# A spectral filter and a SwiGLU block: the last step of the inverse transform on 32x32 tiles of TensorE, one burst a chunk, combined by GpSimd

## The chip, the cores and the metric

One Trainium2 chip, one NeuronCore of it. The metric is the device time of one execution in microseconds, taken as the median of several runs; beside the runs there is one execution recorded by the profiler, and all durations come from that one. The engines are called TensorE (PE in the profile, its weight loads PEld), VectorE (DVE), ScalarE (ACT), GpSimd (POOL) and SyncE (SP, which here only issues DMAs).

## The reference

```python
batch, seq, dim = (8, 3008, 256)          # n_freq = 1505
n_tokens, d_model, d_ff = (24064, 256, 1536)

def _attn_ref(x, filt_r, filt_i):
    X = np.fft.rfft(x, axis=1)
    F = (filt_r + 1j * filt_i)[None, :, :]
    Y = X * F
    y = np.fft.irfft(Y, n=x.shape[1], axis=1)
    return y.astype(np.float32)

def _moe_ref(x, w_gate, w_val, w_out):    # x: the filtered sequence, as 24064 tokens
    g = x @ w_gate
    silu = g * (1.0 / (1.0 + np.exp(-g)))
    val = x @ w_val
    return (silu * val @ w_out).astype(np.float32)
```

All of it is float32: a transform of length 3008 along the sequence of each of 8 batches, a pointwise product with a filter, the transform back, and then a gated feed-forward block over all tokens.

## The kernel before

**The transforms.** 3008 is 47 x 64 (`N1`, `N2`). The transform and its inverse are each made of a step over 64 and a step over 47, as small matrix products. For batch 0 the steps are done ahead and beside the first groups, in other functions (`stage1`, `stage2a`, `stage2b`, `stage3`), which the change leaves as they are. For batches 1 to 7 they are folded by symmetry and cut into pieces that TensorE does between the matmuls of the batch before: `quads` in steps 0 to 3 (L717, products `wqa`, on 24 rows x 32 columns of the array), `fours` in steps 4 to 10 (L797, products `wqc` and `wqb`, 64 x 64), and last `back` (L1031, products `wpd`), which turns the 24 real and 24 imaginary coefficients of each of 64 residues into 47 tokens. What `back` makes, `y`, is what the feed-forward block reads. `quads` and `fours` make the next batch, `back` mostly the batch that is being worked on.

**Chunks, groups, steps.** A batch is cut into 4 chunks of tokens (`NCHUNK`), the hidden dimension into 3 groups (`NG`). A step is one group of one chunk, so there are 12 steps a batch and 96 in all; step s of a batch is chunk s // 3 and group s % 3. A chunk's `y` tile is [128, 8, 188]: four parts of the tokens' values and four combinations of them.

**The order within a step** is written out by hand in `SCHEDULE` (L88), as a list of tokens that is walked once a step (L1502). All instructions are pinned: every engine does its own in the order in which the tokens issue them. A token with a prime belongs to the group of the step before. Those which matter here:

- `P0`..`Q3`, `A..`, `B..`, `E..`: the products of the hidden layer (L1125), by a scheme that needs fewer products than the plain one and more sums. `P`/`Q` read `y` and write banks `wk`; `A`, `B` write `wa`, `E` writes `we`.
- `f0`, `f1`, `f2`: ScalarE copies of `wk`; `D01`, `D02`, `D12`: their differences on GpSimd; `s..`, `x..`: sums on VectorE that start a bank `wa` (`s01` reads `D01`); `g`, `u`, `h`, `v`: the activation on ScalarE and its product on VectorE, into tiles `h`.
- `S00`, `S01`, `S10`, ... `S31` (L1173): sums and differences over the tiles `h`, on GpSimd. The first digit is the kind, the second one of the two tiles. S0 is an addition, and S1, S2 and S3 are subtractions that follow from it or from each other.
- `W1`..`W7`: the projection out (L1223, banks `wA`, `wF`, `wG`), two products each, one of each `h` tile. `W6` reads what `S10'` and `S11'` wrote, `W7` what `S20'` and `S21'` wrote.
- `o1`..`o7`: the projections' results are added into the output tile by VectorE; `x0.o` ..: stores of it.
- `n1`, `n2`, `n3`: sums over the next chunk's `y` (`combine_sequence`), on GpSimd, at the end of a chunk's last step.
- `b0`..`b7`: the next piece of the step's burst (`quads`, `fours`, or `first_fold` in step 11); `t0.0` .. `t4.3`: the next piece of one of the step's other pieces.

TensorE has eight PSUM banks, handed out in the order in which they come free.

**`back` before.** A chunk is made in two halves m = 0, 1. The table `back_t` holds for each half 32 of the 47 tokens, tokens 0 to 31 and tokens 15 to 46 (`LATER` is 15), so that 17 are made twice. The 48 coefficients, cosine and sine parts together, are one contraction of 48 rows; the two kinds h of residues lie at partitions 0 and 64. A half has 16 products into two banks, two transposes on VectorE (L1049) from the banks straight into `y`, and after the second half four small sums on GpSimd (128 x 188, `y<-y`). In steps 1, 4 and 7 the first half stands at `t2.0`, the second at `t3.1` (L1473), for the chunk that begins two steps later; chunk 0 of the next batch is done in step 11 from `t0.0` on (L1471). `load_t4` (L664) brings the coefficients of a chunk in two tiles, with two DMAs each on SyncE's queue. The tiles `x` of `xpool` (two buffers of [128, 512]) are used in batches 0 and 1 only.

Of the kernel before, what the change touches and what calls it, by code (L numbers as in the profile page):

```python
# [41 lines left out]
FP32 = mybir.dt.float32  # L42
# [43 lines left out]


SCHEDULE = """  # L88
Q0 o3' z1.o' t4.2' W2 b0 f0 S00' S01' i0 b1 b2 x0.o' t0.0 x1.o' i1 Q1 P0 t0.1 x2.o' P3 x3.o' f1 t4.3'
W1 x4.o' S10' x03 S11' D01 i2 i3 i4 s13 b3 x5.o' P1 o1 b4 t0.2 o2 z0.o c1 i5 A13 g1 c0 S20' Q2  # L90
S21' g0 y01 m13 t1.0 h0 f2 s01 W6 t1.1 h1 x23 D02 P2 o6 D12 A01 t0.3 i6 c2 i7 B13 i8 g2 i9 n3' m01
i10 S30' t1.2 i11 x02 W7 S31' g13 y12 y02 B01 h13 o7 t1.3 t2.0 s02 s12 g01 h2 b5 Q3 t2.1 h01 e12
A02 y23 W4 e02 b6 y03 m02 g3 A12 o4 z2.o t2.2 E12 m12 B02 t2.3 l12 e13 b7 E02 u12 g02 t3.0 h3 s23
l02 B12 v12 E13 t3.1 h02 u02 A23 n2 l13 g12 v02 W5 s03 e23 h12 e01 m23 A03 o5 z3.o u13 E23 t3.2 m03
v13 E01 l23 e03 t3.3 t4.0 l01 u23 B23 v23 u01 E03 n1 t4.1 v01 g23 B03 l03 W3 h23 g03 u03 h03 v03
""".split()
KS = (-1, 0, 1, 2)

# [15 lines left out]
LATER = N1 - 32  # L114

PIECES = ((0, 7), (7, 14), (14, 20), (20, 26))

# [4 lines left out]
def dft_tables():  # L122
# [27 lines left out]
    hi = 2 * np.pi * (np.outer(2 * n1 + 1, s) % (2 * N1)) / (2 * N1)  # L150
    scale = np.where(s == 0, 1.0, 2.0) / S
    one_hi = np.concatenate([np.cos(hi) * scale, -np.sin(hi) * scale * (s > 0)], 1).T
    back = np.zeros((128, 2, 32))
    for h, table in enumerate((one, one_hi)):
        for m in range(2):
            back[64 * h:64 * h + 2 * NS, m] = table[:, LATER * m:LATER * m + 32]
    back = back.reshape(128, 64)

    quad = np.zeros((4, 32, 2, 32))
    for h in range(2):  # L160
# [40 lines left out]
def kernel(  # L201
# [357 lines left out]
    def load_back():  # L559

        t = rpool.tile([128, 2, 128], U32, name="quad", tag="pw", bufs=3)
        t = t.bitcast(FP32).rearrange("p b f -> p (b f)")
        quad_t.append(t)
        pin(nc.sync.dma_start(out=t[:, 0:65], in_=quad_dram.ap()))
        t = rpool.tile([128, 2, 128, 2], U32, name="back", tag="raw", bufs=2)
        t = t.bitcast(FP32).rearrange("p b f two -> p (b f two)")
        back_t.append(t[:, 0:64])
        pin(nc.sync.dma_start(out=back_t[0], in_=back_dram.ap()))


# [1 line left out]
    def bank(name):  # L572
        return wps.tile([128, 512], FP32, name=f"w{name}", tag="w")
# [7 lines left out]
    class Spectral:  # L581
# [82 lines left out]
        def load_t4(self, k, i, part=None):  # L664
            at = 2 * k + i
            if part:
                self.load_rows(self.t4[k, i][8 * N_STORED:NK], k, slice(2 * N_STORED, NS), ts(i, NH))
                return
            t = t4pool.tile([128, NH, C], FP32, name=f"t4_{self.b}_{k}_{i}", tag="t4")
            if part == 0:  # L670
                self.load_rows(t[0:8 * N_STORED], k, slice(0, 2 * N_STORED), ts(i, NH), nc.gpsimd)
            elif self.b == 0:
                self.load_rows(t[0:NK], k, slice(0, NS), ts(i, NH))
            else:

                rows = self.d2_tokens.rearrange("(h n) a c -> h a n c", h=2)
                for h in range(2):
                    self.load(out=t[64 * h:64 * h + 2 * NS], in_=rows[h, :, ts(at, NH)])
            self.t4[k, i] = t

        def bank(self, name):
# [346 lines left out]

        def back(self, k, m):  # L1031

            if m == 0:
                self.y[k] = ypool.tile([128, 8, TQ], FP32, name=f"y_{self.b}_{k}", tag="y")
            y = self.y[k]
            banks = [bank(f"pd_{self.b}_{k}_{m}_{h}") for h in range(2)]
            outs_ = [t.rearrange("p (z i n d) -> p i z n d", z=2, i=2, d=32) for t in banks]
            for i in range(2):
                t = self.t4[k, i].rearrange("p n (z j d) -> p j z n d", z=2, d=32)
                for j in range(4):  # L1040
                    for h in range(2):
                        r = slice(64 * h, 64 * h + 2 * NS)
                        pin(nc.tensor.matmul(  # L1043
                            out=outs_[h][32 * j:32 * j + 32, i], lhsT=back_t[0][r, ts(m, 32)],
                            rhs=t[r, j], start=i == 0, stop=True, skip_group_check=True))
            yield
            to = y.rearrange("p s n -> p (s n)").rearrange("p (z h m r) -> p h z m r", z=2, h=2, r=N1)
            for h in range(2):
                pin(nc.vector.transpose(  # L1049
                    out=to[:, h, :, :, LATER * m:LATER * m + 32],  # L1050
                    in_=banks[h].rearrange("p (z m d) -> p z m d", z=2, d=32)))
                if h == 0:
                    yield
            for a in range(4 if m else 0):
                b, v = y[:, a], y[:, 4 + a]
                for _ in range(abs(KS[a])):
                    pin((sub if KS[a] > 0 else add)(nc.gpsimd, v, v, b))
# [33 lines left out]
    class Group:  # L1091
# [94 lines left out]
        def project(self, op, last=False):  # L1186
# [9 lines left out]
            if kind in "xXi":  # L1196
                t, cb, step = outs[b, k], int(kind == "X"), 2 if last else 1
                if kind == "x" and q < NG - 1 and takes_turns(b, k) and p == 5:
                    pin(nc.sync.dma_start(out=o_dram[k], in_=t))
                if q == NG - 1 and (b or kind == "i"):  # L1200
                    some = (p,) if kind == "i" else (2 * p, 2 * p + 1)
                    for n, (u, cq) in enumerate(divmod(m, 4) for m in some):
                        rows = min(32, NR - 32 * u)
                        at = (b * S + 32 * 32 * u + 2 * NH * k) * C + 128 * cb + 32 * cq
                        queue = nc.sync if b else nc.gpsimd
                        if last:
                            queue = (nc.sync, nc.scalar, nc.gpsimd)[(2 * p + n) % 3]
# [164 lines left out]


    older = before = None
    gap = iter(())
    pieces_before = []

    def order_of(b):
# [24 lines left out]
            yield  # L1403


    def later(piece):

        yield
        yield from piece

    def chain(*pieces):

# [30 lines left out]
    for b in range(B):  # L1443
# [2 lines left out]
        plan = [[] for _ in range(NCHUNK * NG)]  # L1446

        def three(s, k, cur=cur):
            if s.b == 0:
                return [s.stage3(k, step) for step in range(4)]  # L1450
            return [s.back(k, m) for m in range(2)]

        d = [three(cur, k) for k in range(1, NCHUNK)]
# [7 lines left out]
        if b + 2 < B:  # L1461
            bursts[-1] = following.first_fold()
        bursts = [iter(p) for p in bursts]
        two = []
        for u in range(N_TWO + 2) if b == 0 else ():
# [1 line left out]
            two += [nxt.stage2a(u)] if u < N_TWO else []  # L1467
        if nxt:
            gap = iter(())
            first = three(nxt, 0)  # L1470
            plan[11] = [first[0], gap, first[1]]  # L1471
            if b:
                plan[1], plan[4], plan[7] = [[gap, gap, p[0], later(p[1])] for p in d]  # L1473
            if b == 0:
                for k in range(NCHUNK - 1):
                    plan[k] = d[k] + one[k:k + 1]
                plan[0] = [gap, d[0][0], chain(d[0][1], d[0][2]), d[0][3], one[0]]
                plan[3], plan[4], plan[5] = one[3:8], one[8:13], one[13:16]
# [3 lines left out]
        else:  # L1482
            plan[1], plan[4], plan[7] = [[gap, gap, p[0], later(p[1])] for p in d]

        for step in range(NCHUNK * NG + (b == B - 1)):
            ghost = step == NCHUNK * NG
# [15 lines left out]
            for place, token in enumerate(SCHEDULE):  # L1502
# [51 lines left out]
                if op in ends and not last and (b or step >= NT * NG - 1):  # L1554
                    reload_weights((g + 1) % NG, ends[op])
            older, before, pieces_before = before, this, pieces
    for op in LAST:
        if op[0] == "S":
            older.step(op, nc.gpsimd if op[1] == "2" else nc.vector)
# [30 lines left out]
```

## Time and profile before

| What | Value |
|---|---|
| Median of 3 runs | 2785.24 us (2785.04 to 2791.29) |
| The profiled execution's own time | 2790.41 us |
| Its span, first to last instruction | 2788.6 us |
| Mean granted TensorE clock | 0.997 |
| L1043 weight loads, `wpd<-t,back` 48x32 | x1792, 27.5 us busy |
| L1049 VectorE transposes, `y<-wpd`, 128x512 | x112, 79.2 us busy, 707 ns each |
| L315 GpSimd `D<-f,f` 128x376 | x288, 280.5 us busy, 985 ns each |
| L877 GpSimd `lent<-lent` 128x512 | x48, 60.4 us busy, 1278 ns each |
| Time that GpSimd's `h` (L312) waited for VectorE's `h` | 402.2 us, 62 times |

A row of the groups reads: line, engine, operation, out <- in, partitions x elements, count, then busy time in us, the mean of one in ns, the idle time of the engine just before these instructions, and what ended it. Line numbers can be those of a helper: L312 is every addition, L315 every subtraction. A row of the timeline has the start in us, the duration of the merged run, the engine and the instruction. A row of windows has for each stretch its length, the busy time of PE, PEld, DVE, ACT and POOL with the number of instructions, the granted clock, the DMA share and GB/s. One product in float32 leaves two records on TensorE.

### The profile page before, as it was taken

What the parts mean: (1) busy time and instruction counts of PE and PEld (TensorE: products, weight loads), DVE (VectorE), ACT (ScalarE), POOL (GpSimd) and SP (SyncE); (2) the same over time, 40 slices, a digit from 0 to 9 for tenths busy, and PEclk for the clock granted to TensorE, in tenths of its full rate; (3) what the DMA queues carried; (4) which work ended last, traced back from release to release, by engine and by line L of the source; (5) the groups of instructions that cost most, each with busy time, mean ns of one, the idle gap of its engine ahead of it and who ended that gap; (6) DMA issues with size and microseconds to landing.
All of it is one profiled execution on the core that took longest, in us unless ns stands there. A gap on an engine that the chain in (4) does not pass through costs nothing.

```text
span 2788.6 us, 51410 instructions
## 1 busy us (share of the span) xinstructions
PE 2748.3 (99%) x16952; PEld 2249.3 (81%) x16952; DVE 2081.7 (75%) x4703; ACT 1514.6 (54%) x4086; POOL 1647.4 (59%) x1801
## 2 busy tenths in 40 slices
PE   8999999999999999999999999999999999999998
PEld 6777887888878888788878888878887888888886
DVE  7888777777687777777778777777777777676666
ACT  5776454555555555555555555555554555555553
POOL 4786576566545665556654566555655566555554
PEclk9999999999999999999999999999999999999999
DMA  8688877878676776777767777668767677655543
GB/s 216 218 273 267 282 240 243 265 243 263 205 211 208 253 244 190 212 238 229 247 184 233 220 249 223 207 194 264 243 213 201 215 239 237 183 156 147 156 137 83
DMA packets 383488, 608.47 MB, mean 218 GB/s; under 512 B 197118, under 2 KB 266652, under 8 KB 383048
## 3 DMA queue, kind: packets, MB, share of 16 engines
q1 hardware_dynamic: 364410, 574.18, 65.9%
q10 hardware_dynamic: 16174, 25.50, 3.6%
q0 software_dynamic: 2640, 5.51, 0.7%
q8 instruction: 137, 2.24, 0.3%
q14 instruction: 127, 1.04, 0.1%
HBM read 484.45 MB, written 118.12 MB: 216 GB/s over the span
## 4 chain that ended last, share of the span: by engine, by line
PE 89%; DVE 3%; POOL 2%; ACT 1%; DMA 1%; issue 1%; SPq 0%; POOLq 0%; DVEq 0%; ACTq 0%
PE wa L1125 25%; PE wk L1125 17%; PE wA L1223 16%; PE we L1125 12%; PE wG L1223 8%; PE wF L1223 4%; PE wpd L1043 2%; PE wqc L807 1%; PE wqb L819 1%; PE wqa L727 1%; POOL h L315 0%; POOL out_dram L1208 0%; PE wpa L889 0%; DVE we L315 0%; DVE y L319 0%
## 5 line engine op out<-in xcount | busy, mean ns | idle before, releaser
L1125 PE MATMUL wa<-y_t,wt_t 128*128 128x188 f32 x4464 | 883.5, 324 | 10.5 <-DVE wa L1147 5.5
L1125 PEld LDWEIGHTS wa<-y_t,wt_t 128*128 128x128 f32 x4464 | 746.0, 190 | 102.9 <-issue 14.7
L1125 PEld LDWEIGHTS wk<-y,wt_t 128*128 128x128 f32 x2976 | 494.4, 190 | 125.2 <-issue 36.7
L1125 PE MATMUL wk<-y,wt_t 128*128 128x188 f32 x2976 | 575.6, 326 | 1.4 <-ACT f L1140 1.4
L315 POOL TENSOR_TENSOR h<-h 128x376 f32<-128x376 f32 x572 | 560.1, 1000 | 15.1 <-DVE h L312 14.9
L1223 PE MATMUL wA<-h,wo_t 128*128 128x376 f32 x1532 | 549.0, 481 | 3.4 <-POOL h L315 1.8
L1125 PE MATMUL we<-y_t,wt_t 128*128 128x188 f32 x2232 | 432.4, 323 | 2.4 <-DVE we L319 1.6
L315 POOL TENSOR_TENSOR D<-f,f 128x376 f32<-128x376 f32 x288 | 280.5, 985 | 252.0 <-ACT f L1140 245.4
L312 POOL TENSOR_TENSOR h<-h 128x376 f32<-128x376 f32 x190 | 183.2, 984 | 408.0 <-DVE h L1172 402.2
L315 DVE TENSOR_TENSOR we<-we,m 128x376 f32<-128x376 f32 x576 | 317.3, 552 | 91.6 <-PE we L1125 51.4
L1125 PEld LDWEIGHTS we<-y_t,wt_t 128*128 128x128 f32 x2232 | 369.1, 190 | 4.9 <-DVE we L319 2.8
L1223 PEld LDWEIGHTS wA<-h,wo_t 128*128 128x128 f32 x1532 | 278.0, 190 | 106.6 <-POOL h L315 5.4
L1160 ACT COPY m<-wa 128x376 f32<-128x376 f32 x576 | 275.4, 478 | 110.8 <-PE wa L1125 105.0
L1167 ACT ACTIVATE u<-we 128x188 f32<-128x188 f32 x576 | 188.9, 328 | 188.5 <-DVE we L315 179.1
L1223 PE MATMUL wG<-h,wo_t 128*128 128x376 f32 x768 | 273.9, 479 | 0.0
L319 DVE SCALAR_TENSOR_TENSOR y<-wk,c 128x376 f32<-128x376 f32 x480 | 246.7, 540 | 33.7 <-ACT c L1144 29.5
L1167 ACT ACTIVATE g<-wa 128x188 f32<-128x188 f32 x576 | 187.4, 326 | 143.8 <-PE wa L1125 141.6
L1144 ACT COPY c<-wk 128x376 f32<-128x376 f32 x288 | 136.9, 475 | 234.5 <-PE wk L1125 228.1
L1156 ACT COPY we<-y 128x376 f32<-128x376 f32 x480 | 218.9, 480 | 42.9 <-DVE y L1049 24.7
L1140 ACT ACTIVATE f<-wk 128x376 f32<-128x376 f32 x288 | 145.1, 504 | 168.6 <-PE wk L1125 108.3
L1172 DVE TENSOR_TENSOR h<-we,u 128x188 f32<-128x188 f32 x576 | 198.7, 345 | 35.1 <-ACT u L1167 21.9
L1172 DVE TENSOR_TENSOR h<-wa,g 128x188 f32<-128x188 f32 x576 | 196.1, 344 | 26.2 <-ACT g L1167 26.1
(194 smaller groups left out, 3532.0 us busy)
## 6 DMA issues: line engine op xcount, KB each, us to landing
wt_t<-w_all SPq DMA_DIRECT2D x174, 896.0 KB
wt_t<-w_all SPq DMA_DIRECT2D x174, 768.0 KB
lent<-filter SPq DMA_DIRECT2D x36, 1024.0 KB
quads<-lent SPq DMA_DIRECT2D x96, 256.0 KB
d<-lent ACTq DMA_DIRECT2D x84, 256.0 KB
t<-d SPq DMA_DIRECT2D x112, 192.0 KB
lent<-quads SPq DMA_DIRECT2D x144, 128.0 KB
lent<-raw SPq DMA_DIRECT2D x144, 128.0 KB
```

The costliest lines, as they stand in the source:

```text
L312: return eng.tensor_tensor(out=dst, in0=a, in1=b, op=ALU.add)
L315: return eng.tensor_tensor(out=dst, in0=a, in1=b, op=ALU.subtract)
L319: return nc.vector.scalar_tensor_tensor(out=dst, in0=a, scalar=-1.0, in1=b, op0=ALU.mult, op1=ALU.subtract)
L1043: pin(nc.tensor.matmul(out=outs_[h][32 * j:32 * j + 32, i], lhsT=back_t[0][r, ts(m, 32)], rhs=t[r, j], start=i == 0, stop=True, skip_group ...
L1125: pin(nc.tensor.matmul(out=ps[:, z], lhsT=self.wt[:, SLOT[p], z], rhs=rhs, start=start and z == 0, stop=True, skip_group_check=True))
L1140: pin(act.mul(self.small(f"f{i}", f"f{i}", 1), t[f"k{i}"], -1.0))
L1144: pin(act.copy(out=self.small(f"c{i}", f"c{i}", 1), in_=t[f"k{i}"]))
L1156: pin(act.copy(out=self.bank(f"e{at}"), in_=t[f"y{at}"]))
L1160: pin(act.copy(out=self.small(f"m{at}", "m", 4), in_=t[f"a{at}"]))
L1167: pin(act.activation(out=self.small(op, "g", 3, 1)[:, 0], in_=ps[:, 1], func=AF.Silu))
L1172: pin(v.tensor_tensor(out=dst, in0=ps[:, 0], in1=g, op=ALU.mult))
L1223: pin(nc.tensor.matmul(out=self.tiles[at], lhsT=wo_t[:, JB * q + i, WO[p], :], rhs=self.hs[i][:, HID[p]], start=start and i == 0, stop=Tru ...
```

## The change

`back` makes a chunk in one burst. Cosine and sine parts are contracted apart, each with 24 rows, and only for 24 of the 47 tokens; the two kinds of residues and the two parts lie at partitions 0, 32, 64 and 96 and fill four banks. VectorE transposes each bank into a tile `turn` of `xpool` (two buffers), and GpSimd writes the sum of cosine and sine part as the first 24 tokens and the difference, in reverse order, as the other 23. In the schedule three tokens are new: `r0` before `W3` at a step's end (the burst), `r1'` after `o3'` and `r2'` after `t4.2'` (two transposes, an addition and a subtraction each), `r3'` after `f1` (the four small sums). They act on chunk k with the burst in step 3k - 2, that is 1, 4, 7. Chunk 0 of the next batch takes `b0` to `b3` of step 11, side by side with `first_fold`. A tile of coefficients is loaded with four DMAs. In the last drain the stores of the second column half use two queues in turn, SyncE's and ScalarE's, for three.

```diff
-Q0 o3' z1.o' t4.2' W2 b0 f0 S00' S01' i0 b1 b2 x0.o' t0.0 x1.o' i1 Q1 P0 t0.1 x2.o' P3 x3.o' f1 t4.3'
+Q0 o3' r1' z1.o' t4.2' r2' W2 b0 f0 S00' S01' i0 b1 b2 x0.o' t0.0 x1.o' i1 Q1 P0 t0.1 x2.o' P3 x3.o' f1 r3' t4.3'
 W1 x4.o' S10' x03 S11' D01 i2 i3 i4 s13 b3 x5.o' P1 o1 b4 t0.2 o2 z0.o c1 i5 A13 g1 c0 S20' Q2
 S21' g0 y01 m13 t1.0 h0 f2 s01 W6 t1.1 h1 x23 D02 P2 o6 D12 A01 t0.3 i6 c2 i7 B13 i8 g2 i9 n3' m01
...
-v13 E01 l23 e03 t3.3 t4.0 l01 u23 B23 v23 u01 E03 n1 t4.1 v01 g23 B03 l03 W3 h23 g03 u03 h03 v03
+v13 E01 l23 e03 t3.3 t4.0 l01 u23 B23 v23 u01 E03 n1 t4.1 v01 g23 B03 l03 r0 W3 h23 g03 u03 h03 v03
...
-    back = np.zeros((128, 2, 32))
+    back = np.zeros((4, 32, 32))
     for h, table in enumerate((one, one_hi)):
-        for m in range(2):
-            back[64 * h:64 * h + 2 * NS, m] = table[:, LATER * m:LATER * m + 32]
-    back = back.reshape(128, 64)
+        back[2 * h:2 * h + 2, 0:NS, 0:NS] = table.reshape(2, NS, N1)[:, :, 0:NS]
+    back = back.reshape(128, 32)
...
-                rows = self.d2_tokens.rearrange("(h n) a c -> h a n c", h=2)
-                for h in range(2):
-                    self.load(out=t[64 * h:64 * h + 2 * NS], in_=rows[h, :, ts(at, NH)])
+                rows = self.d2_tokens.rearrange("(h n) (r s) c -> h r s n c", h=2, r=2)
+                for part in range(4):
+                    self.load(out=t[32 * part:32 * part + NS],
+                              in_=rows[part // 2, part % 2, :, ts(at, NH)])
...
-        def back(self, k, m):
-
-            if m == 0:
-                self.y[k] = ypool.tile([128, 8, TQ], FP32, name=f"y_{self.b}_{k}", tag="y")
-            y = self.y[k]
-            banks = [bank(f"pd_{self.b}_{k}_{m}_{h}") for h in range(2)]
+        def back(self, k):
+
+            self.y[k] = y = ypool.tile([128, 8, TQ], FP32, name=f"y_{self.b}_{k}", tag="y")
+            banks = [bank(f"pd_{self.b}_{k}_{part}") for part in range(4)]
+            views = [t.rearrange("p (z i n d) -> p i z n d", z=2, i=2, d=32) for t in banks]
             for i in range(2):
                 t = self.t4[k, i].rearrange("p n (z j d) -> p j z n d", z=2, d=32)
                 for j in range(4):
-                    for h in range(2):
-                        r = slice(64 * h, 64 * h + 2 * NS)
+                    for part in range(4):
+                        r = slice(32 * part, 32 * part + NS)
                         pin(nc.tensor.matmul(
-                            out=outs_[h][32 * j:32 * j + 32, i], lhsT=back_t[0][r, ts(m, 32)],
+                            out=views[part][32 * j:32 * j + 32, i], lhsT=back_t[0][r],
                             rhs=t[r, j], start=i == 0, stop=True, skip_group_check=True))
             yield
             to = y.rearrange("p s n -> p (s n)").rearrange("p (z h m r) -> p h z m r", z=2, h=2, r=N1)
             for h in range(2):
-                pin(nc.vector.transpose(
-                    out=to[:, h, :, :, LATER * m:LATER * m + 32],
-                    in_=banks[h].rearrange("p (z m d) -> p z m d", z=2, d=32)))
-                if h == 0:
-                    yield
-            for a in range(4 if m else 0):
+                both = []
+                for part in (2 * h, 2 * h + 1):
+                    t = xpool.tile([128, NV, C], FP32, name=f"turn_{self.b}_{k}_{part}", tag="x")
+                    t = t.rearrange("p i c -> p (i c)")
+                    pin(nc.vector.transpose(out=t, in_=banks[part]))
+                    both.append(t.rearrange("p (z m r) -> p z m r", z=2, r=32))
+                first = 1 - h
+                for f, there, n in ((add, to[:, h, :, :, 0:NS], slice(0, NS)),
+                                    (sub, to[:, h, :, :, N1 - 1:NS - 1:-1],
+                                     slice(first, first + N1 - NS))):
+                    pin(f(nc.gpsimd, there, both[0][:, :, :, n], both[1][:, :, :, n]))
+                yield
+            for a in range(4):
                 b, v = y[:, a], y[:, 4 + a]
                 for _ in range(abs(KS[a])):
                     pin((sub if KS[a] > 0 else add)(nc.gpsimd, v, v, b))
...
-                            queue = (nc.sync, nc.scalar, nc.gpsimd)[(2 * p + n) % 3]
+                            queue = (nc.sync, nc.scalar, nc.gpsimd)[(2 * p + n) % (3 - cb)]
...
+    def side_by_side(*pieces):
+
+        for _ in range(8):
+            for piece in pieces:
+                next(piece, None)
+            yield
...
+        backs = {3 * k - 2: cur.back(k) for k in range(1, NCHUNK)} if b else {}
...
+            bursts[-1] = side_by_side(nxt.back(0), following.first_fold() if b + 2 < B else gap)
...
-            first = three(nxt, 0)
-            plan[11] = [first[0], gap, first[1]]
-            if b:
-                plan[1], plan[4], plan[7] = [[gap, gap, p[0], later(p[1])] for p in d]
...
+                elif op[0] == "r":
+                    next(back_before if old else backs.get(step, gap), None)
```

More of the change, by code (lines that the diff above doesn't have):

```diff
@@ L112 @@
 NPR = len(ORDER)
-LATER = N1 - 32
 PIECES = ((0, 7), (7, 14), (14, 20), (20, 26))
@@ L566, in load_back @@
         t = t.bitcast(FP32).rearrange("p b f two -> p (b f two)")
-        back_t.append(t[:, 0:64])
+        back_t.append(t[:, 0:32])
         pin(nc.sync.dma_start(out=back_t[0], in_=back_dram.ap()))
@@ L1027, in stage3 @@
                         out=v, in0=b, scalar=-float(k), in1=c, op0=ALU.mult, op1=ALU.add))
-        def back(self, k, m):
-            if m == 0:
-                self.y[k] = ypool.tile([128, 8, TQ], FP32, name=f"y_{self.b}_{k}", tag="y")
-            y = self.y[k]
-            banks = [bank(f"pd_{self.b}_{k}_{m}_{h}") for h in range(2)]
-            outs_ = [t.rearrange("p (z i n d) -> p i z n d", z=2, i=2, d=32) for t in banks]
+        def back(self, k):
+            self.y[k] = y = ypool.tile([128, 8, TQ], FP32, name=f"y_{self.b}_{k}", tag="y")
+            banks = [bank(f"pd_{self.b}_{k}_{part}") for part in range(4)]
+            views = [t.rearrange("p (z i n d) -> p i z n d", z=2, i=2, d=32) for t in banks]
             for i in range(2):
@@ L1374 @@
     older = before = None
-    gap = iter(())
+    gap = back_before = iter(())
     pieces_before = []
@@ L1403, in sooner @@
             yield
-    def later(piece):
-        yield
-        yield from piece
+    def side_by_side(*pieces):
[3 more added lines that the diff above has]
+            yield
     def chain(*pieces):
@@ L1448, in three @@
         def three(s, k, cur=cur):
[L1449 to L1453, printed above, removed]
+            return [s.stage3(k, step) for step in range(4)]
+        d = [three(cur, k) for k in range(1, NCHUNK)] if b == 0 else []
+        backs = {3 * k - 2: cur.back(k) for k in range(1, NCHUNK)} if b else {}
         one = [] if b else [nxt.stage1(u) for u in range(N_ONE)]
@@ L1460 @@
                 bursts[N_QUAD // 2 + n] = nxt.fours(n)
-        if b + 2 < B:
-            bursts[-1] = following.first_fold()
+        if nxt:
+            bursts[-1] = side_by_side(nxt.back(0), following.first_fold() if b + 2 < B else gap)
         bursts = [iter(p) for p in bursts]
@@ L1481 @@
                 plan[6][0] = sooner(plan[6][0])
-        else:
-            plan[1], plan[4], plan[7] = [[gap, gap, p[0], later(p[1])] for p in d]
         for step in range(NCHUNK * NG + (b == B - 1)):
@@ L1556 @@
             older, before, pieces_before = before, this, pieces
+            back_before = backs.get(step, gap)
     for op in LAST:
```

## The prediction

> **What bounds the kernel now.** I read the page first: busy shares, then the chain of waits.
>
> ```profile
> PE 2748.3 (99%) x16952; PEld 2249.3 (81%) x16952; DVE 2081.7 (75%) x4703; ACT 1514.6 (54%) x4086; POOL 1647.4 (59%) x1801
> ...
> PE 89%; DVE 3%; POOL 2%; ACT 1%; DMA 1%; issue 1%; SPq 0%; POOLq 0%; DVEq 0%; ACTq 0%
> ```
>
> TensorE is busy almost without a break, and the chain that ended last is TensorE for 89%. A microsecond taken off TensorE is gained; one that TensorE must wait is lost, as nothing later makes it up. GpSimd is free for 41% of the span, but what matters is where. Next, the groups of instructions, shapes apart, of TensorE and of GpSimd.
>
> ```profile
> L1043 PE MATMUL wpd<-t,back 48*32 48x256 f32 x1792 | 61.4, 382 | 0.0
> ...
> L727 PE MATMUL wqa<-lent,quad 24*32 24x512 f32 x768 | 27.4, 600 | 0.0
> ```
>
> ```profile
> L315 POOL TENSOR_TENSOR h<-h 128x376 f32<-128x376 f32 x572 | 560.1, 1000 | 15.1 <-DVE h L312 14.9
> ...
> L315 POOL TENSOR_TENSOR y<-y 128x188 f32<-128x188 f32 x84 | 49.9, 608 | 35.0 <-DVE y L1049 32.8
> ```
>
> The last step of the transforms (L1043) has 1792 records, two for a product: 56 bursts of 16 products, two bursts a chunk. Then the timeline of TensorE and of GpSimd where step 4 of batch 3 ends and step 5 begins, the place to which the burst is moved.
>
> ```profile
> 1256.41 1.43 PE L1223 MATMUL wG<-h,wo_t 128*128 128x376 f32 x4
> 1257.67 0.80 PE L1125 MATMUL wk<-y,wt_t 128*128 128x188 f32 x4
> ...
> 1259.67 1.09 PE L807 MATMUL wqc<-lent 64*64 64x256 f32 x16
> 1260.58 1.04 PE L819 MATMUL wqb<-lent 64*64 64x256 f32 x16
> 1261.55 2.18 PE L1125 MATMUL wk<-y,wt_t 128*128 128x188 f32 x12
> 1263.57 1.43 PE L1223 MATMUL wA<-h,wo_t 128*128 128x376 f32 x4
> ...
> 1266.74 1.43 PE L1223 MATMUL wA<-h,wo_t 128*128 128x376 f32 x4
> ```
>
> ```profile
> 1257.53 1.91 POOL L312 TENSOR_TENSOR h<-h 128x376 f32<-128x376 f32 x2 [0.38 <-DVE h L1172]
> 1259.41 1.95 POOL L315 TENSOR_TENSOR h<-h 128x376 f32<-128x376 f32 x2
> 1263.39 0.98 POOL L315 TENSOR_TENSOR D<-f,f 128x376 f32<-128x376 f32 x1 [2.03 <-ACT f L1140]
> 1264.33 1.93 POOL L315 TENSOR_TENSOR h<-h 128x376 f32<-128x376 f32 x2
> ```
>
> The first row is W3; call its start T. The wA at 1266.74 is W6, and its second product (1267.37) reads what S11', the last GpSimd operation of the second row, wrote by 1261.36: 6.02 us in hand. The same pair has 5.23 us where the next step opens with a quads burst, 3.92 in the last batch, which has neither quads nor fours, and 5.28 in a step 11.
>
> **TensorE's gain.** From a burst's first record to the next matmul is 1.024 us in 55 of 56 bursts, and the first comes 0.252 after its forerunner where the usual pitch is 0.160. So a burst costs 1.024 + 0.092 = 1.12, a chunk 2.23. The new burst has as many products (32, 64 records of 256 columns), but on 32x32 tiles. The nearest row is L727: 24x32, 32 records of 512 columns in 1.071 us, the same number of columns, entered with the same extra 0.09. A chunk then costs 1.16, and 28 chunks save 28 x 1.07 = 30 us. From above: were the records as close as L1043's 34 ns and no closer, 64 of them would take 2.2 us and nothing is saved.
> [...]
>
> **What stays.** The four transposes a chunk remain (L1049, 128x512, 0.709 us each, pitch 0.63 among other work), now into a 512-wide buffer of which there are two. The four small sums of 128x188 (pitch 0.60) remain. Each of 56 input loads becomes four issues for two, of half the bytes: 112 more in SP's queue. SP's waits are mostly for TensorE (996 us in L477's), and the loads land at least 6.1 us ahead wherever the trace ties them to a burst but the first; eight issues took 3.82 us at the end, so four more cost 2 us of that. I take nothing; uncovered, 1 us a chunk. In the last drain four output stores leave GpSimd's queue for SP's and ScalarE's; at 0.5 to 0.6 us an issue that is within 1.3 us either way. I take 0.
>
> **What is added, and to what it is queued.** GpSimd gets four sums a chunk, of 384 and 368 elements in pieces of 24 and 23. No row has such pieces. Lower end 0.95 us (pitch of the 128x376 rows), upper end 1.28 (128x512, L877, were the gaps of the 32-wide rows paid too). I take 0.95, by the number of elements; the upper end adds 1.3 us a chunk, 37 in all. Their work is no matter; their place is. In the order of the built program all four stand ahead of S00' in GpSimd's queue, and each pair waits for two transposes, which stand behind o3', which waits for W3, which now stands behind the burst. The third transpose waits for the first pair, since only two buffers exist. With T the burst's start:
> - burst to 1.17, then W3; o3' starts 1.46 after W3 as now: 2.63. Transposes at 3.10 and 3.73, done 4.44.
> - GpSimd, 0.08 later: first pair 4.52 to 6.46.
> - Third and fourth transpose 6.51 to 7.85. Second pair 7.93 to 9.87.
> - S00', S01' (1.88 for two) to 11.71; now they end at T + 3.0.
> - The four small sums (r3' stands before S10') to 14.1; S10', S11' to 16.05; now T + 4.95.
> W6's second product is due at 10.96 + 1.17 = 12.13 and starts at 16.1: TensorE loses 4.0 us. D01 ends at 17.0, s01 on VectorE at 17.58, and A01, due 17.4, loses 0.2 more. S20', S21' (18.9) are then in time for W7. So 4.2 us in steps 5 and 8 of six batches: 12 x 4.2 = 50. After a step 1 followed by quads, W6 is due 11.35: 6 x 4.75 = 28. Last batch, due 10.05, and A01 0.25: 3 x 6.3 = 19. Chunk 0, in step 11 (time from Q0; there S00', S01' come first): transposes done 4.57, pair to 6.59, transposes to 7.98, pair to 10.0, S11' to 11.9 where W6 needs it at 8.88: 3.1; then D01, the small sums at b3 to 15.2, S21' to 17.15 where W7 needs it at 15.5: 1.7. 7 x 4.8 = 34. Sum: 131 us.
> On the way TensorE also waits for a bank: Q1, due 6.31, needs the third transpose (7.22); VectorE's x03 and s13 stand behind the fourth. These lie inside the same 4 to 6 us.
>
> **The clock.** Windows of the trace's start show what a poorly used stretch does.
>
> ```profile
> 8.80:12.22 3.42, 1.89 (x18) 1.72 (x16) 2.08 (x6) 1.24 (x3) 0.00 (x0) 1.00 1.07 233
> 12.22:15.63 3.41, 3.41 (x19) 3.41 (x17) 1.65 (x6) 1.40 (x3) 0.81 (x2) 0.50 1.04 243
> ...
> 22.46:25.87 3.41, 3.41 (x28) 3.17 (x28) 0.57 (x2) 2.78 (x5) 0.00 (x0) 1.00 1.08 321
> ```
>
> After 3.41 us in which TensorE was idle 1.53 us (and streamed columns for some 36%, at the 0.85 ns a column of 188 in 0.160 us), the granted clock is 0.50 for 10.24 us, three such windows; no later window streams under 42% before the last drain, and the clock stays 1.00 until then. In the new order W6 is preceded by an idle stretch of 2.7 us (Q1 having waited 0.9 before it), and the last batch's Q1 waits 2.9. Such a stretch leaves 36% or less of a window in about half of all phases: (3.41 - 2.7 + 2 x (2.7 - 2.18)) / 3.41 = 0.51. Of 24 stretches 12 cost a window at half clock, 1.7 us each: 21 us. Bounds: 0, and three windows each, 63.
> [...]
>
> Sum: 131 - 30 + 21 = +122. On the profiled span, 2788.6 + 122 = 2911. That execution took 2790.41, 5 us over the median of the runs; on the median it is 2785.24 + 122 = 2908.
>
> **Rivals.**
> - The stalls without a loss of clock: 131 - 30 = +101, 2887. [...] Chance 0.25.
> - Three windows at half clock an event: 131 - 30 + 63, 2950. For it: the only halving shown lasted 10.24 us. Against: TensorE was thinly used all through that stretch. Chance 0.14.
> - The change doesn't do what it says: 32x32 tiles no faster, burst 2.2 us. The 30 us fall away, 2938. Against: L727. Chance 0.05.
> - A new wait takes the place, but a smaller one: GpSimd's delay fits the slack, and only the banks and VectorE's queue behind the two buffers are left: 0.9 x 12 + 1.7 x 6 + 2.9 x 3 + 1.9 x 7 = 43, less 30: 2798. It needs the four sums at under half a microsecond. Chance 0.05.
> - Faster: TensorE's 30 us are kept, 2755. One mechanism: W6's 6.02, 5.23, 3.92 us in hand cover GpSimd's delay. For it: GpSimd is 59% busy and waits 402 us in all for S00's operands. Against: the delay is 16.05 - 4.95 - 1.17 = 9.9 us, of which the sums themselves are 3.8. It decides once the chain to S11' is 3.5 us shorter on average. Chance 0.08.
>
> **The numbers.** Main case 0.43, 2908. Its own bounds: 2887 without the clock, and 11 less at 0.85 us a sum; 2945 at 1.28. The range goes from 2840 to 2960, leaving out the faster case, the one with banks alone and the far ends. About 0.3% (8 us) is what a measurement of this kernel can tell from no change. Faster 0.08; of the bank case 0.02 lies within 0.3%; slower 0.90.
>
> **What would show it.** Of after: 28 bursts at the place of L1043, each some 1.07 us to the next matmul (else the gain is wrong). wA (W6) with an idle time before it of 60 to 100 us in all, put down to GpSimd's h; wk with some 30, put down to VectorE's transposes. GpSimd busy some 110 us more. The third transpose 2 us after the second. PEclk under 9 in slices, or a mean clock of 0.98 to 0.99, if the clock term is right. I am wrong if wA's row shows no idle time, or if TensorE's share of busy time stays at 99%.

## The result and the profile after

| | before | after |
|---|---|---|
| Median of 4 runs each, side by side | 2786.84 us (2785.04 to 2791.29) | 2935.84 us (2934.48 to 2937.48) |
| Span of the profiled execution | 2788.6 us | 2932.7 us |
| Mean granted TensorE clock | 0.997 | 0.979 |

The ratio is 1.0532, with an interval of 1.0514 to 1.0551: 149 us slower, where 122 were forecast. The page's busy shares and its chain of waits:

```profile
PE 2792.3 (95%) x16952; PEld 2274.4 (78%) x16952; DVE 2093.7 (71%) x4703; ACT 1506.2 (51%) x4086; POOL 1748.6 (60%) x1909
...
PE 74%; POOL 10%; DVE 5%; DMA 3%; issue 1%; ACT 1%; SPq 1%; DVEq 0%; POOLq 0%; ACTq 0%
```

TensorE was busy for 99% of the span and is busy for 95% of a longer one; on the chain it falls from 89% to 74%, and GpSimd rises from 2% to 10%, though its own busy time grew by only 101 us. The groups, shapes apart, say where TensorE stands still (the last columns are the idle time ahead of the group and what ended it), first in the kernel before, then in the changed one:

```profile
L1125 PE MATMUL wk<-y,wt_t 128*128 128x188 f32 x2976 | 575.6, 326 | 1.4 <-ACT f L1140 1.4
L1223 PE MATMUL wA<-h,wo_t 128*128 128x376 f32 x1532 | 549.0, 481 | 3.4 <-POOL h L315 1.8 <-DVE o L312 1.4
```

```profile
L1226 PE MATMUL wA<-h,wo_t 128*128 128x376 f32 x1532 | 586.5, 505 | 72.1 <-POOL h L312 68.5 <-DVE o L309 2.8
L1128 PE MATMUL wk<-y,wt_t 128*128 128x188 f32 x2976 | 588.2, 332 | 19.7 <-DVE turn L1049 19.7
```

`wA` (its `W6`) had 3.4 us of idle time before and has 72.1, of which 68.5 are put down to GpSimd's `h`, which here is `S10'` and `S11'`; `wk` (`Q1`) waits 19.7 us for VectorE's transposes. Line numbers have shifted by two or three. The spot below is of the same kind as the prediction's, one chunk later: step 7 of batch 3 ends and step 8 begins, with a `fours` burst like step 5's. First TensorE, then GpSimd and VectorE:

```profile
1392.90 1.50 PE L1039 MATMUL wpd<-t,back 24*32 24x256 f32 x64
1394.32 1.53 PE L1226 MATMUL wG<-h,wo_t 128*128 128x376 f32 x4
...
1400.47 2.18 PE L1128 MATMUL wk<-y,wt_t 128*128 128x188 f32 x12 [0.83 <-DVE turn L1049]
...
1408.17 2.87 PE L1226 MATMUL wA<-h,wo_t 128*128 128x376 f32 x4 [2.35 <-POOL h L312]
```

```profile
1397.74 1.00 POOL L309 TENSOR_TENSOR y<-turn,turn 128x384 f32<-128x384 f32 x1 [12.30 <-DVE turn L1049]
1398.69 0.97 POOL L312 TENSOR_TENSOR y<-turn,turn 128x368 f32<-128x368 f32 x1
1401.09 0.99 POOL L309 TENSOR_TENSOR y<-turn,turn 128x384 f32<-128x384 f32 x1 [1.43 <-DVE turn L1049]
...
1402.98 1.91 POOL L309 TENSOR_TENSOR h<-h 128x376 f32<-128x376 f32 x2
...
1407.14 1.94 POOL L312 TENSOR_TENSOR h<-h 128x376 f32<-128x376 f32 x2
```

```profile
1396.35 1.31 DVE L1049 STREAM_TRANSPOSE turn<-wpd 128x512 f32<-128x512 f32 x2
1399.70 1.32 DVE L1049 STREAM_TRANSPOSE turn<-wpd 128x512 f32<-128x512 f32 x2 [2.04 <-POOL y L312]
```

With T = 1392.90 the transposes run from 3.45 to 4.76, the first pair of sums to 6.76, the second transposes from 6.80 (VectorE waited 2.04 us for the pair, since there are two buffers), the second pair to 10.12, `S00'` and `S01'` to 11.99, `S10'` and `S11'` to 16.18. W6 stands still for 2.35 us ahead of its first product and waits once more inside its 2.87 us.

Compared step by step with the kernel before, every step that issues a burst at its end is 0.82 us shorter; steps 5 and 8 of batches 1 to 6 are 5.2 to 5.6 us longer, their step 2 some 6.1, the three of the last batch 7.8 to 8.5, and every step 11 from 4.7 to 6.5. All other steps of batches 1 to 7 agree within 0.02 us.

### The profile page after: what moved, and what is told of

Read it like the earlier page. It is cut to its first block, busy times and chain, and to the rows that moved or that the text cites. A ratio compares the mean times of both kernels' runs of the same rounds, so it can differ in the third digit from the quotient of the medians.

```text
span 2932.7 us, 51561 instructions
## 1 busy us (share of the span) xinstructions
PE 2792.3 (95%) x16952; PEld 2274.4 (78%) x16952; DVE 2093.7 (71%) x4703; ACT 1506.2 (51%) x4086; POOL 1748.6 (60%) x1909
## 3 DMA queue, kind: packets, MB, share of 16 engines
q14 instruction: 129, 1.05, 0.1%
## 4 chain that ended last, share of the span: by engine, by line
PE 74%; POOL 10%; DVE 5%; DMA 3%; issue 1%; ACT 1%; SPq 1%; DVEq 0%; POOLq 0%; ACTq 0%
PE wa L1128 22%; PE wA L1226 15%; PE wk L1128 12%; PE we L1128 11%; PE wG L1226 7%; POOL y L312 3%; PE wF L1226 3%; POOL y L309 2%; POOL h L312 2%; POOL h L309 1%; DVE turn L1049 1%; PE wpd L1039 1%; PE wqc L805 1%; DMA lent<-in_x_dram 1%; PE wqb L817 1%
## 5 line engine op out<-in xcount | busy, mean ns | idle before, releaser
L1128 PE MATMUL wa<-y_t,wt_t 128*128 128x188 f32 x4464 | 889.8, 326 | 23.0 <-DVE wa L1150 14.5
L1128 PEld LDWEIGHTS wa<-y_t,wt_t 128*128 128x128 f32 x4464 | 755.0, 192 | 110.0 <-issue 16.9
L1226 PE MATMUL wA<-h,wo_t 128*128 128x376 f32 x1532 | 586.5, 505 | 72.1 <-POOL h L312 68.5
L1128 PEld LDWEIGHTS wk<-y,wt_t 128*128 128x128 f32 x2976 | 512.3, 195 | 141.8 <-issue 38.0
L1128 PE MATMUL wk<-y,wt_t 128*128 128x188 f32 x2976 | 588.2, 332 | 19.7 <-DVE turn L1049 19.7
L309 POOL TENSOR_TENSOR y<-turn,turn 128x384 f32<-128x384 f32 x56 | 55.8, 997 | 357.7 <-DVE turn L1049 357.7
```

Source lines behind the costliest of these rows:

```text
L309: return eng.tensor_tensor(out=dst, in0=a, in1=b, op=ALU.add)
L1128: pin(nc.tensor.matmul(out=ps[:, z], lhsT=self.wt[:, SLOT[p], z], rhs=rhs, start=start and z == 0, stop=True, skip_group_check=True))
L1226: pin(nc.tensor.matmul(out=self.tiles[at], lhsT=wo_t[:, JB * q + i, WO[p], :], rhs=self.hs[i][:, HID[p]], start=start and i == 0, stop=Tru ...
```

## The experiments

A step's loss below is its length less its length in the kernel before, from the two traces. The ratios are to the kernel before, run beside each.

**1. Queue order and buffers, apart and together.** The first takes `S00'` to `S11'` ahead of the four sums; the list is the same for every step:

```diff
-Q0 o3' r1' z1.o' t4.2' r2' W2 b0 f0 S00' S01' i0 ...
-W1 x4.o' S10' x03 S11' D01 ...
+Q0 o3' S00' S01' S10' S11' r1' z1.o' t4.2' r2' W2 b0 f0 i0 ...
+W1 x4.o' x03 D01 ...
```

> Only the order is changed: S00' S01' S10' S11' stand ahead of the four sums in GpSimd's queue. Theory A (the sums' place in GpSimd's queue delays S11' and so W6): S11' ends about 6.2 us after the burst's start, in time for W6 (due at 12.1); what is left is TensorE's wait at Q1 for a bank, because the third transpose now waits for the first pair until 8.2 and Q1 is due at 6.3: some 1.5 us in 12 steps, 2.3 in 6, 3.4 in 3 and 2.2 in 7, 57 us; less 20 us that the bursts save: 2822 us (2800 to 2845), wA with next to no idle time, few windows at half clock. Rival B (the two buffers and the banks make the loss, the order little): 2900 or more. Rival C (GpSimd simply has too much work): 2936, as the changed kernel.

Measured: 2836.49 us, 1.0152 (1.0132 to 1.0173). The second gives the transposes three and four two tiles of their own (the table `back_t` moves beside `quad_t`, which frees them):

```diff
-t = xpool.tile([128, NV, C], FP32, name=f"turn_...", tag="x")
+if h:
+    t = rpool.tile([128, 2, 128, 2], U32, name=name, tag="raw", bufs=2)
+else:
+    t = xpool.tile([128, NV, C], FP32, name=name, tag="x")
```

> Only the buffers are changed: four turn tiles a chunk in place of two, so that no transpose waits for a pair of sums; the order is that of the change. Theory A: S11' comes only some 1.4 us earlier (14.8 us after the burst's start for 16.2), W6 still loses 2.7 us in 12 steps, 3.5 in 6, 4.8 in 3 and 1.7 in 7, 79 us, less 20, and some windows at half clock: 2860 us (2840 to 2890). wk no longer waits for VectorE's turn (19.7 us before this edit, then under 3). Rival B: the two buffers make the loss, so the time falls to 2790 or less.

Measured: 2889.34 us, 1.0351 (1.0332 to 1.0369). The third has both edits.

> Both: S00' to S11' ahead of the sums, and four turn tiles. Theory A: neither W6 nor Q1 waits any more, the small sums end some 12.4 us after the burst's start and D01 at 13.3, in time for A01; what is left is the burst's gain of some 20 us: 2767 us (2755 to 2785), faster than the kernel before. Rival C (GpSimd's 110 us more of work, wherever it stands) or rival D (the burst's place at the step's end, which delays W3 and what reads it): above 2800.

Measured: 2796.65 us, 1.0018 (1.0007 to 1.0028). The two groups of TensorE that waited, by shape, in the first, the second and the third kernel:

```profile
L1128 PE MATMUL wk<-y,wt_t 128*128 128x188 f32 x2976 | 574.2, 326 | 19.7 <-DVE turn L1049 19.7
L1226 PE MATMUL wA<-h,wo_t 128*128 128x376 f32 x1532 | 551.8, 482 | 9.6 <-POOL h L312 6.0 <-DVE o L309 3.2
```

```profile
L1131 PE MATMUL wk<-y,wt_t 128*128 128x188 f32 x2976 | 578.2, 327 | 1.7 <-ACT f L1146 1.7
L1229 PE MATMUL wA<-h,wo_t 128*128 128x376 f32 x1532 | 568.4, 490 | 75.0 <-POOL h L312 70.0 <-DVE o L309 3.2
```

```profile
L1131 PE MATMUL wk<-y,wt_t 128*128 128x188 f32 x2976 | 572.6, 325 | 1.8 <-ACT f L1146 1.8
L1229 PE MATMUL wA<-h,wo_t 128*128 128x376 f32 x1532 | 551.8, 482 | 8.8 <-POOL h L312 5.2 <-DVE o L309 3.2
```

Each edit takes away its own wait and leaves the other: the order ends the wait for GpSimd's `h` (68.5 to 6.0), the buffers the wait for VectorE's `turn` (19.7 to none). By the ratios the order alone recovers some 106 of the 149 us, the buffers alone some 50, both together some 143. So theory A holds as to which wait is which, and rivals B and C fall; D too, as the burst stands where the change put it. The sizes were missed: the buffers alone came out 29 us above the expectation, since a step 11 still lost 4.4 us on average, net of the burst's gain, where about 1 was expected, and order and tiles together 30 above it (5 us of both are the kernel before, which ran at 2792 beside them). In the third kernel the steps 5 and 8 lose 0.03 us, as expected, but a step 11 still 2.6 to 3.1 in five of seven, net of the burst's gain. In batch 3's, 1.1 us arise at W7, which waits for `S20'` and `S21'` behind the small sums, and 2.3 behind W7.

**2. The sums on VectorE**, with the change's order and its two buffers:

```diff
-pin(f(nc.gpsimd, there, both[0][...], both[1][...]))
+pin(f(nc.vector, there, both[0][...], both[1][...]))
```

> The order and the two buffers are those of the change, but the four sums are done by VectorE, not by GpSimd. Theory A: GpSimd has only the small sums ahead of S10', S11' ends near 9 us after the burst's start, W6 doesn't wait; VectorE does some 2.2 us more a chunk ahead of x03 and s13, which delays a few products: 2785 us (2765 to 2810). Rival D (the burst's place makes the loss) : 2900 or more. Rival E (VectorE becomes the bound in these steps, as it has the transposes and the sums ahead of x03): 2810 to 2880, with wa waiting for VectorE.

Measured: 2814.32 us, 1.0077 (1.006 to 1.0094). The wait for `h` is gone (3.2 us), and 31.4 us of idle time ahead of `wa` are put down to VectorE's `wa` (14.5 in the changed kernel): the work moves the queue's trouble to the other engine. Theory A's range is missed by 4 us; rival E, in its range, is right that VectorE then holds TensorE up.

**3. The small sums behind all that is urgent**, on top of order and tiles:

```diff
-... x3.o' f1 r3' t4.3'
+... x3.o' f1 t4.3'
...
-... o6 D12 A01 ...
+... o6 D12 r3' A01 ...
...
+for _ in range(0 if k else 2):
+    yield
 for a in range(4):
```

> On top of the new order and the four turn tiles, the four small sums are moved behind D12 (and in step 11 to the last piece of the burst, behind S21'). The version with order and tiles alone came out at 1.002 of the kernel before, 0.8 us better in each of the steps after a burst except 0.54 and 0.99 us lost in 6 and 3 of them and some 2.8 us in each step 11, where W7's S20' and S21' stand behind the small sums. Theory A (all that is lost is what waits in GpSimd's queue): the losses go, every delayed step costs nothing, and the whole gain of the bursts, 20 us, is left: ratio 0.993 (0.990 to 0.996). Rival C/D (the work or the burst's place costs something of its own, in step 11 above all, through VectorE's queue): ratio 0.998 to 1.003.

Measured: 2777.18 us, 0.9951 (0.9938 to 0.9964), faster than both kernels. Of the three steps behind a burst two lose 0.03 us, the one with quads 0.4; a step 11 is within 0.8 us of before. In the groups next to nothing is left of the two waits:

```profile
L1133 PE MATMUL wk<-y,wt_t 128*128 128x188 f32 x2976 | 574.8, 326 | 0.0
L1231 PE MATMUL wA<-h,wo_t 128*128 128x376 f32 x1532 | 548.1, 480 | 2.1 <-DVE o L309 1.9 <-POOL h L312 0.2
```

It is 14 us better than before and not 20. What is missing is in steps 2 (6 x 0.4) and 11 (the burst's gain does not show there).

**4. The burst cut in two**, on top of that: 16 products ahead of W3, 16 behind it.

```diff
-... B03 l03 r0 W3 h23 ...
+... B03 l03 r0 W3 r0 h23 ...
...
+                if k and i == 0:
+                    yield
```

> As the kernel with the small sums last, but a chunk's burst (chunks 1 to 3) is cut in two: 16 products ahead of W3 and 16 behind it. In the burst of 64 records the first 32 start 7 ns apart and the last 32 16.6 ns. If the slow half comes from the number of records in a row (a supply of instructions that runs dry), both halves run at 7 ns: each costs some 0.5 us, a chunk 1.0 to 1.2 for 1.52, so 0.3 us a chunk less, 7 us in all. If it comes from the second half itself (it accumulates into banks that sixteen tiles already write), the pitch stays 16.6 ns in the second half, a chunk costs as much as before or 0.1 us more for the second entry, and the time is the same or 2 us longer.

Measured: 2780.02 us, 0.9966 (0.9955 to 0.9977). TensorE in the timeline of that kernel:

```profile
2512.18 0.71 PE L1037 MATMUL wpd<-t,quad 24*32 24x256 f32 x32
2512.82 1.53 PE L1233 MATMUL wG<-h,wo_t 128*128 128x376 f32 x4
2514.28 0.71 PE L1037 MATMUL wpd<-t,quad 24*32 24x256 f32 x32
2514.92 0.90 PE L1135 MATMUL wk<-y,wt_t 128*128 128x188 f32 x4
```

Both halves now start their records 7 ns apart, so the 17 ns of the long burst's second half do not come from accumulating; of the two explanations the number of records in a row is left. But each half takes 0.64 us to the next matmul, 0.30 of them after its last start, and is entered with 0.09 extra: 2 x 0.736 = 1.47 us a chunk against 1.52, where 1.0 to 1.2 was expected. The first product behind a burst is 0.10 us slower as well, now twice a chunk; by the step lengths a cut chunk costs 0.06 us more than an uncut one. The 7 us do not come.

**5. The wait filled.** The changed kernel, with work of no use ahead of W6 in steps 2, 5, 8 and 11, into columns of the bank that nothing reads:

```diff
+if op == "W6" and this and (b > 0 and step in (2, 5, 8) or b < B - 1 and step == 11):
+    for _ in range(7):
+        pin(nc.tensor.matmul(out=g0.unread, lhsT=wo_t[:, 0, 0, :],
+                             rhs=wo_t[:, 1, 0, :], start=False, stop=True, ...))
```

> The changed kernel with its order and its two buffers; in steps 2, 5, 8 and 11 seven products of 128x128 into columns of wA's bank that nobody reads are put ahead of W6, some 1.6 to 2.3 us of TensorE work in the stretch in which it waits for S11' (2.5 us on average). No other work is changed. Clock theory (a window of 3.41 us with 37% or less of streaming is followed by one at half clock, and that lengthens the stretch behind it): the 27 half-clock windows go, S11' comes when it came, and the time falls by 25 to 55 us, to 2881 to 2911. Rival (the half clock falls on stretches in which TensorE waits anyway, and costs nothing): 2936 or a little more.

Measured: 2930.23 us, 1.05 (1.0485 to 1.0514), some 9 us below the changed kernel by the ratios, whose intervals just touch. The same spot in the timeline:

```profile
1406.35 1.73 PE L1537 MATMUL wA<-wo_t 128*128 128x128 f32 x14
1408.88 1.85 PE L1228 MATMUL wA<-h,wo_t 128*128 128x376 f32 x4 [0.80 <-POOL h L312]
```

Leaving out the first 100 us and the drain, the windows at half clock fall from 27 stretches of 109 us in all to 5 of 17; three of the five are in steps 2, 5 and 8 of the last batch. The mean clock rises from 0.979 to 0.996; W6 takes 1.85 us for 2.87. Yet the expected 25 to 55 us do not come. In steps 5 and 8 the full clock saves 0.8 us each (5.36 to 4.55 on average), in the last batch 0.5 each, and steps 2 and 11 even become 0.4 and 0.2 us longer: there VectorE, late by then, holds TensorE up in the second half of the step instead (1.45 us of step 2's 6.53 arise behind W7). That loss goes with one addition of VectorE, here in step 2 of batch 3:

```profile
1239.34 0.97 POOL L309 TENSOR_TENSOR y_t<-y 128x376 f32<-128x376 f32 x1
1239.37 1.50 DVE L309 TENSOR_TENSOR lent<-lent 128x512 f32<-128x512 f32 x1
```

It starts 0.03 us behind the start of an addition of GpSimd and takes 1.50 us. In this run's six such steps 2 it took 1.49 to 1.51 us each time, and 1.44 to 1.46 us are lost behind W7. In the changed kernel's six it took 0.68 us, and nothing is lost there; in batch 3 it is all but over when GpSimd's addition starts, as that waits 0.66 us for TensorE. So the half clock that went had cost 7 us net by the steps, 9 by the ratios; the rival has most of it.

**6. The same extra work in two places.** Each pair of sums issued twice, once where the change has them and once, in the kernel of experiment 3, behind D12:

```diff
-pin(f(nc.gpsimd, there, ...))
+for _ in range(2):
+    pin(f(nc.gpsimd, there, ...))
```

> The changed kernel with its order and two buffers, each pair of sums issued twice in its place: 112 more GpSimd instructions, some 110 us more of its time (it is idle for about 40%). Theory A (what stands ahead of S11' in GpSimd's queue is paid for by TensorE, one for one): S11' comes 3.9 us later in each of 28 steps, 109 us in all: 3045 us (3025 to 3075). Rival C (the sums are too much work, wherever they stand): the same here, so the twin run tells.

Measured: 3059.85 us, 1.096 (1.0943 to 1.0976), some 120 us above the changed kernel and within theory A's range.

```diff
...
+for f, there, cosine, sine in again:
+    pin(f(nc.gpsimd, there, cosine, sine))
 for a in range(4):
```

> The kernel with the small sums last, and the same 112 instructions more, but ahead of the small sums, behind all that W6, A01 and W7 need. Theory A: nothing waits for them in 21 steps; in the seven steps 11 they end close before the sums over y, 0 to 2 us each: 2777 to 2795 us, no more than 15 us over the kernel without them. Rival C (GpSimd's work as such): 110 us over it, 2890.

Measured: 2796.21 us, 1.0018 (1.0007 to 1.003), some 19 us above the kernel of experiment 3. The same 112 instructions cost about 120 us in the one place and about 19 in the other; the place decides, as theory A has it, and the 19 are a little more than it allowed. The first kernel has the change's two buffers as well and the second four tiles: in the first, TensorE's wait for `turn` grows from 19.7 to 57.7 us and the mean clock falls to 0.959, so its 120 us are not all a wait for `S11'`. The 19 don't fall in step 11 as expected (0.3 us each there) but in step 2 (1.4) and in steps 5 and 8 (0.4), and in the last batch, where VectorE has no folds (`lent<-lent`, sums for the next batch) to do, they are nothing. The groups of VectorE, first in the kernel before, then in this one:

```profile
L312 DVE TENSOR_TENSOR lent<-lent 128x512 f32<-128x512 f32 x48 | 36.1, 753 | 4.6 <-DMA lent<-in_x_dram 4.5
...
L877 DVE TENSOR_TENSOR lent<-lent 128x512 f32<-128x512 f32 x24 | 16.4, 683 | 0.0
```

```profile
L309 DVE TENSOR_TENSOR lent<-lent 128x512 f32<-128x512 f32 x48 | 50.1, 1043 | 4.2 <-DMA lent<-in_x_dram 4.2
...
L873 DVE TENSOR_TENSOR lent<-lent 128x512 f32<-128x512 f32 x24 | 28.6, 1192 | 0.0
L312 DVE TENSOR_TENSOR lent<-lent,wqc 128x512 f32<-128x512 f32 x36 | 24.8, 688 | 66.3 <-ACT lent L838 66.3
```

VectorE's sums with both operands in SBUF grow from 753 to 1043 ns and from 683 to 1192; those with one operand in PSUM (`lent<-lent,wqc`) took 688 before and take 688 here. Part of the growth is older than the second set of sums: in the kernel of experiment 3 the same two groups stand at 912 and 869.

## Why the prediction was right, and where it was not

The forecast was 2908 us, slower, by GpSimd's queue; it came to 2936. Its mechanism was right, and the sum was too small, by errors of both signs.

- **TensorE's gain: 30 us forecast, 23 measured.** The burst takes 1.425 us to the next matmul, not 1.07; with the entry, 1.52 a chunk for 2.23. By the step lengths a chunk gains 0.82 us, and 28 x 0.82 = 23. The 0.1 between the two is a term that the prediction lacked: the first product behind a burst is slower (W3's second record comes 0.42 us after its first, for 0.32), twice a chunk before and once now. The step that failed is the nearest row: L727 has 32 records of 512 columns, and the same number of columns was taken for the same time. In the burst of 64 records the first half starts 7 ns apart, the second 17 ns.
- **The chain from the burst to S11': right.** Forecast ends against measured ones, in us after T: first pair 6.46 and 6.76, second pair 9.87 and 10.12, S01' 11.71 and 11.99, S11' 16.05 and 16.18. The sums' 0.95 us each are the pitch measured (1398.69 - 1397.74). Experiments 1 and 6 show that it is the queue that makes the loss.
- **The stalls: 131 us forecast, some 160 measured** where the clock doesn't disturb. Experiment 5 gives them, each step against before, with the 0.82 us of step 11's own burst added: 12 x 4.55 + 6 x 6.53 + 47 for the seven steps 11, and some 3 x 6.3 for the last batch. The last term is an estimate: those steps lost 7.61 us, but at half clock still. `s01` ended 17.7 us after T in all three, and A01 started at 18.7 to 18.9, where it follows in 0.15 us in the other batches' steps; that and A01's own first products make some 1.3 us of clock. So the last batch's 6.3, and the 0.25 for A01 in it, were right. So are steps 5 and 8 where they were worked out: at W7 the delay is 4.16 us, for 4.2 forecast. The step that failed is the end of the sum at W7: behind it come 0.38 us in steps 5 and 8, 1.45 in step 2, and in step 11 2.3 in six batches and 0.6 in the last one, of which the prediction, which followed GpSimd, has nothing: 12 x 0.38 + 6 x 1.45 + 6 x 2.3 + 0.6 = 28 of the 29.
- **What was costed at nothing.** The doubled number of loads shows as 0.2 us ahead of `wpd`, put down to a DMA. The drain's queues gave nothing: the last 32 us of the two traces, which hold all of the drain, agree in length within 0.02 us. No run had that edit alone.
- **The clock: 21 us forecast, some 11 measured**: 7 net by experiment 5 and, by the estimate above, 4 for the last batch's three windows, which stayed there. 27 stretches came, not 12: one in every step 2, 5 and 8 behind a burst, 21 in all, so the phases fell worse than half, and one in six of the seven steps 11, which the prediction did not count. The failing step is the price: 1.7 us a window assumed that TensorE was the bound for all of it. Windows around the spot show why it isn't:

```profile
1404.65:1408.07 3.42, 1.17 (x8) 0.88 (x6) 1.58 (x4) 1.99 (x6) 3.34 (x6) 1.00 0.51 168
1408.07:1411.48 3.41, 3.31 (x7) 2.10 (x8) 1.43 (x4) 0.00 (x0) 3.41 (x5) 0.50 0.78 245
```

  The columns are the window and its length, then the busy time of PE, PEld, DVE, ACT and POOL, and the granted clock. In the halved window VectorE is busy for 1.43 us and GpSimd throughout: `D01` ends at 1410.01 and `s01` at 1410.61, so `A01` waits for them at any clock: it started 17.86 us after T in experiment 5 and 18.90 here, 1.04 lost and not 1.7. In steps 2 and 11 the window cost nothing on balance: without it TensorE ran into VectorE's slow addition (experiment 5).

  In the window ahead of the halving TensorE was busy for 1.17 us. Without the clock term the forecast would have been some 11 us too low in it; with it, it was 10 too high. So 10 us of the total's nearness are luck: the clock's excess made up for a part of what the stalls lacked.
- **The sum.** 160 - 23 + 11 = 148, the sum of the step lengths, against 149 between the medians and 144 between the spans; ahead of step 11 of batch 0, which has the first burst, the profiled execution of the changed kernel was 3.6 us faster. The 27 us by which the forecast was low are 29 more of stalls and 7 less of gain, less 10 of clock.
- **The rivals.** The 32x32 tiles do gain, so that one falls. The rival with banks alone, 2798, needed sums of under half a microsecond, and they take 0.95; its wait is there as a second one, and experiment 1 shows what it costs once GpSimd's delay is gone (42 us over the kernel before, where the transposes come later still than the rival had them). The faster rival gave 2755 with all waits covered; the best version found runs at 2777.

What stays open: the loss behind W7 in steps 2 and 11 goes with VectorE's one slow addition in the traces of the changed kernel and of experiment 5. In the changed kernel's steps 11, four with that addition at 1.5 us lose 2.3 us behind W7, two with it at 0.68 lose 0.75, and the one without folds 0.6. But no run moved that addition alone, so the traces show that the two come together and no experiment shows that one causes the other; in the third kernel of experiment 1 a step 2 loses 0.5 us behind W7 with the addition at 0.68. The last 0.6 to 0.75 us of step 11 and the 0.38 of steps 5 and 8 are not explained.

## What to carry to other kernels

Before work is given to an engine because it is half idle, look at what stands behind it in that engine's queue and by when TensorE needs it: some 110 us of GpSimd time cost about 120 us ahead of an urgent sum and about 19 behind it, and one reordered line with two more buffers turned a loss of 5.3% nearly into nothing. Follow the delay to the end of the step, not to the first engine that catches up. A clock that drops while TensorE waits for others can cost much less than its length: here 109 us at half clock cost some 11.

## What the runs showed of the hardware

- **VectorE beside GpSimd.** Sums of 128x512 with both operands in SBUF took 683 to 753 ns on average, by group, in the kernel before, 950 for one of the groups in the changed kernel, and 817 to 1192 in the second kernel of experiment 6; those with a PSUM operand took 675 to 692 in all of them. Of the first kind, those that no GpSimd instruction overlapped took 669 to 692 ns in the traces of the kernel before and the changed one, and the slowest of the others 1.21 us in the first and 1.51 in the second.
- **A long burst of small products.** The first 32 records of a burst on 32x32 tiles start 7 ns apart, with a gap of 140 ns in the middle; the next 32 start 17 ns apart, behind two gaps of 0.12 and 0.19 us (27 of the 28 bursts of the changed kernel). Two bursts of 32 with a projection between them (experiment 4) took 0.71 us each; they run at 7 ns, with the gap of 140 ns in the middle of each. Of the two explanations of experiment 4 that leaves the number of records in a row; what lies behind it no run shows.
- **The clock.** In the traces of the kernel before and the changed one, the changes of the granted clock lie on a grid of 3.413 us. A share of streaming is an estimate from the columns of TensorE's records at 0.85 ns each (188 in 0.160 us). By it, all 27 stretches at half clock of the changed kernel, behind the first 100 us and ahead of the drain, follow a window in which TensorE streamed 37% or less, and of the windows there that the full clock followed, the least streamed 43%. The first 100 us of the same trace show that this is no sharp line: the window from 66.63 us streamed some 48%, and two at half clock followed it.
